# Two attention units from one 512-token load, all scores ahead of the first product with v, narrow idle matmuls first, and a last tile in three column pieces

## The chip, the cores and the metric

The kernel runs on one core of one Trainium2 chip. The metric is device time in microseconds (us); lower is better. Times are medians of several executions. Ratios are the mean time of one kernel's fast runs over that of the other's fast runs of the same rounds, so they are not quite the ratio of the medians quoted. A time is some 1.8 us longer than the span in the profile of the same run.

Words used below: TensorE (PE) does the matmuls and also loads their weights (PEld); VectorE is DVE, ScalarE is ACT, GpSimd is POOL. An *idle matmul* is one whose result nobody reads; it is there only to keep TensorE's clock up (run e8: with 25 of the 39 removed, the granted clock was at half from 12.4 to 19.2 us). *pv* is the product of the attention weights with v. *hps* is the hidden layer of the feed-forward part, *ops* its output layer.

## The reference, cut to what matters

```python
# attention inside chunks of 64 tokens, 8 heads of 64, then x @ w_in, a swish with a beta per column, @ w_out
scores = scale * np.matmul(q_c, k_c.transpose(0, 1, 2, 4, 3))
attn = np.exp(scores - max);  attn = attn / (sum + 1e-09)
x = np.matmul(attn, v_c)            # -> 4608 tokens x 512
h = x @ w_in                        # 512 -> 2048
g = h * (1.0 / (1.0 + np.exp(-beta * h)))
out = g @ w_out                     # 2048 -> 512
```

## The kernel before: the parts that matter

Tokens are handled in units of 256 (18 units) and blocks of two units (9 blocks). The order is written by hand. The beginning, with cuts:

```python
        # q, k of unit 0, heads 0-3: plain loads; heads 4-7: converting loads on the GpSimd queue
        for a, eng, dst in ((0, nc.sync, raw0), (1, nc.gpsimd, qk0[1])): ...   # runs of 512 B
        load_qk(1)                      # unit 1: two converting loads
        for i in range(4): load_v(i)
        ...                             # then w_in (8 loads), w_out, later units
        emit_idle(11, 512)              # 11 idle matmuls of 512 columns
        emit_T_half(0); emit_sc_half(0) # transpose on DVE, scores, exp
        emit_idle(3, 512)
        emit_T_half(1); emit_sc_half(1)
        ...
        emit_idle(13, 512)
        emit_T(1, ("qT", "kT")); emit_sc(1)
        emit_idle(4, 512)
        emit_pv(0); emit_norm(0, 0); emit_norm(0, 1)
        emit_idle(3, 512); emit_xt_pe(0, 0); emit_idle(3, 512); emit_xt_pe(0, 1); emit_idle(2, 512)
        emit_pv(1); emit_norm(1, 0); emit_norm(1, 1)
        a0, v0 = emit_m(0, 0, 0, 256, True)   # first hps group
```

In the middle, around units 4 and 5, `emit_T(5)` stands ahead of `emit_norm(4, ...)` on DVE, and `emit_sc(5)` ahead of `emit_t(1, 1, 0, 8)`. At the end the last 128 tokens are done in two halves of 256 columns, the second one evacuated by DVE and stored by ACT's queue.

The softmax here doesn't subtract the row's maximum and nothing guards it: scores larger than these inputs give would overflow.

## Time and profile before

| | before |
|---|---|
| median (lowest to highest of 5) | 291.94 us (291.58 to 292.25) |
| span in the profile | 290.0 us |
| TensorE busy | 283.1 us, 39 idle matmuls among it |
| first hps matmul | 16.03 us |
| first ops matmul | 31.11 us |

The first ops matmul is a good milestone: up to there every version here has done exactly the same useful work, so its start time tells what the head cost. The prediction below shows the busy rows, the stretches and the chain. The first row is the granted clock of TensorE in 40 slices of the span (9 is 90% or more); the others are the DMA queues with packets, megabytes and share of the 16 engines.

```profile
PEclk9999999999999999999999999999999999999999
...
q0 software_dynamic: 101216, 18.10, 84.2%
q1 hardware_dynamic: 40544, 18.24, 34.4%
q8 instruction: 21, 0.34, 0.5%
```

The clock is full in all slices. The third queue looks negligible and I passed over it: 21 packets, 0.34 MB, so 16 KB each. They are instructions.

### The profile page before, as it was taken

The page shows a single profiled execution, that of the slowest core. Times are in us where ns is not written, and L with a number is a line of the kernel's source. Part 1 is how long each engine was busy: PE and PEld are TensorE (multiplying, and loading weights), DVE is VectorE, ACT ScalarE, POOL GpSimd, SP SyncE. Part 2 cuts the span into 40 slices and gives each one's busy share as a digit, 9 for nine tenths or more (in the row PEclk, how much of TensorE's full clock was granted, in tenths as well). Part 3 has the DMA queues.
Part 4 walks back from the last instruction along what each step waited for, and adds up shares of the span by engine and source line. Part 5 has one row for each costly group of instructions (what it writes and reads, how often), then busy time and mean ns, then how long its engine had stood idle before and what let it go on. Part 6 is the DMA issues. An engine that isn't in the chain of part 4 may idle for free.

```text
span 290.0 us, 6476 instructions
## 1 busy us (share of the span) xinstructions
PE 283.1 (98%) x2695; PEld 135.5 (47%) x2695; DVE 139.8 (48%) x252; ACT 146.0 (50%) x224; POOL 97.5 (34%) x126
## 2 busy tenths in 40 slices
PE   7999999999999999999999999999999999999995
PEld 2464445545544444444444444444444444444444
DVE  3477444687366644534454444445453636433300
ACT  3277318783456645454545554455445544444411
POOL 8864569379152985070717070000000000000000
PEclk9999999999999999999999999999999999999999
DMA  9999999999969999999999999946346202100111
GB/s 143 170 196 205 177 176 212 211 161 158 133 98 135 200 168 144 168 151 156 135 123 171 118 158 113 198 65 92 91 107 78 75 36 72 38 36 36 38 72 72
DMA packets 141932, 36.86 MB, mean 127 GB/s; under 512 B 130000, under 2 KB 137424, under 8 KB 141904
## 3 DMA queue, kind: packets, MB, share of 16 engines
q0 software_dynamic: 101216, 18.10, 84.2%
q1 hardware_dynamic: 40544, 18.24, 34.4%
q8 instruction: 21, 0.34, 0.5%
q10 hardware_dynamic: 144, 0.13, 0.1%
q14 instruction: 7, 0.06, 0.1%
HBM read 36.71 MB, written 9.44 MB: 159 GB/s over the span
## 4 chain that ended last, share of the span: by engine, by line
PE 91%; DMA 2%; ACT 2%; DVE 2%; POOL 1%; issue 1%; DVEq 0%; ACTq 0%; POOLq 0%
PE hps L303 43%; PE ops L335 41%; DMA ku<-in_k_dram 2%; PE x L256 2%; PE sc L231 2%; PE sc L218 1%; PE ops L540 1%; ACT xt L288 1%; DVE x L271 1%; ACT sg L313 1%; PE warm L352 1%; POOL h L360 1%; PE xp L287 1%; DVE kT L154 0%; ACT osb L345 0%
## 5 line engine op out<-in xcount | busy, mean ns | idle before, releaser
L317 DVE SCALAR_TENSOR_TENSOR gt<-sg,hps 128x512 f16<-128x512 f32 (+1 forms) x152 | 99.2, 658 | 114.5 <-ACT sg L313 114.4
L313 ACT ACTIVATE sg<-hps,beta 128x512 f32<-128x512 f32 (+1 forms) x152 | 100.4, 665 | 74.7 <-PE hps L303 74.7
L303 PE MATMUL hps<-xt,win 128*128 128x512 f16 (+1 forms) x608 | 136.7, 368 | 0.4 <-ACT xt L288 0.2
L335 PE MATMUL ops<-wout,gt 128*128 128x512 f16 x560 | 131.1, 379 | 0.0
L303 PEld LDWEIGHTS <-win 128*128 128x128 f16 x608 | 57.6, 98 | 61.8 <-issue 0.9
L335 PEld LDWEIGHTS <-gt 128*128 128x128 f16 x560 | 53.8, 98 | 63.3
L345 ACT ACTIVATE osb<-ops 128x512 f32<-128x512 f32 x35 | 20.9, 598 | 44.4 <-PE ops L335 44.4
L110 POOL DMA_DIRECT2D vbig<-in_v_dram x40 | 34.2, 876 | 10.0 <-DMA wout<-in_moe_w_out_dram 4.3
L96 POOL DMA_DIRECT2D qu<-in_q_dram x22 | 18.7, 860 | 41.5 <-DMA qT<-qu 39.0
L271 DVE TENSOR_TENSOR x<-x,rd 128x512 f16<-128x512 f32 (+1 forms) x40 | 25.2, 637 | 1.4
L96 POOL DMA_DIRECT2D ku<-in_k_dram x22 | 18.8, 876 | 0.4 <-DMA ku<-in_k_dram 0.4
L240 ACT ACTIVATE et<-sc 128x1024 f16<-128x1024 f32 (+1 forms) x9 | 7.4, 834 | 10.2 <-PE sc L231 10.2
L352 PE MATMUL warm<-idle 128*128 128x512 f16 x39 | 11.2, 429 | 1.2 <-DVE braw L356 1.2
L267 DVE RECIPROCAL rd<-x 128x8 f32<-128x8 f32 x36 | 7.2, 200 | 8.8 <-PE x L256 8.8
L224 ACT ACTIVATE et<-sc 128x1024 f16<-128x1024 f32 x10 | 10.2, 1015 | 0.0
L256 PEld LDWEIGHTS <-et 64*64 64x64 f16 x576 | 6.1, 107 | 7.4 <-issue 3.8
L102 POOL DMA_DIRECT2D ku<-in_k_dram x10 | 7.7, 772 | 2.5 <-DMA win<-in_moe_w_in_dram 1.3
L102 POOL DMA_DIRECT2D qu<-in_q_dram x10 | 7.7, 781 | 2.4 <-DMA win<-in_moe_w_in_dram 1.4
L288 ACT COPY xt<-xp 128x512 f16<-128x512 f16 x12 | 6.7, 588 | 3.3 <-PE xp L287 3.3
L256 PE MATMUL x<-vbig,et 64*64 64x65 f16 x576 | 8.1, 195 | 0.0
L154 DVE STREAM_TRANSPOSE kT<-ku 128x512 f32<-128x512 f32 x7 | 5.0, 711 | 4.9 <-DMA ku<-in_k_dram 4.9
L553 DVE TENSOR_SCALAR osb<-ops 128x256 f32<-128x256 f32 x1 | 0.4, 424 | 12.5 <-PE ops L540 12.5
(34 smaller groups left out, 60.2 us busy)
## 6 DMA issues: line engine op xcount, KB each, us to landing
out_dram<-osb SPq DMA_DIRECT2D x35, 256.0 KB, 3.2
vbig<-in_v_dram POOLq DMA_DIRECT2D x32, 128.0 KB, 7.9
qu<-in_q_dram POOLq DMA_DIRECT2D x20, 128.0 KB, 6.6
ku<-in_k_dram POOLq DMA_DIRECT2D x20, 128.0 KB, 8.2
win<-in_moe_w_in_dram POOLq DMA_DIRECT2D x8, 256.0 KB, 9.2
wout<-in_moe_w_out_dram POOLq DMA_DIRECT2D x4, 512.0 KB, 12.2
qu<-in_q_dram POOLq DMA_DIRECT2D x4, 256.0 KB, 6.5
ku<-in_k_dram POOLq DMA_DIRECT2D x4, 256.0 KB, 7.3
```

Of the source, the lines that this page charges most:

```text
L96: nc.gpsimd.dma_start(out=tv[off:off + n, sp], in_=src[b, :, s:s + n, :].rearrange("h p d -> p h d"),)
L102: nc.gpsimd.dma_start(out=t[off // 2:(off + n) // 2], in_=src[b, :, s:s + n, :].rearrange("h (p r) d -> p h r d", r=2),)
L110: nc.gpsimd.dma_start(out=vbig[off:off + n, i, :, 0:D], in_=v[b, :, s:s + n, :].rearrange("h p d -> p h d"),)
L224: nc.scalar.activation(out=et, in_=sc, func=ACTF.Exp, scale=scale)
L256: nc.tensor.matmul(out=x[64 * c:64 * c + 64, r, g, 0:D + 1], lhsT=(et[64 * r:64 * r + 64, s, 4 * c + g, :] if u < XU else et[64 * r:64 * r ...
L271: nc.vector.tensor_tensor(out=o, in0=x[:, r, :, 0:D], in1=rd[:, r].to_broadcast(list(o.shape)), op=ALU.mult)
L303: nc.tensor.matmul(out=hps[:, 0:n], lhsT=w_in16[m // 2][:, kk, (m % 2) * 128:(m % 2) * 128 + 128], rhs=xr[:, c0 // CH:(c0 + n) // CH, 2 * ...
L313: nc.scalar.activation(out=sg[:, 0:n], in_=hps[:, 0:n], func=ACTF.Tanh, scale=beta2[:, m:m + 1])
L317: nc.vector.scalar_tensor_tensor(out=gt_t[j][:, m, c0:c0 + n], in0=sg[:, 0:n], scalar=1.0, in1=hps[:, 0:n], op0=ALU.add, op1=ALU.mult,)
L335: nc.tensor.matmul(out=ops, lhsT=gt_t[j][:, kk, t * 128:(t + 1) * 128], rhs=w_out16[kk // 4][:, kk % 4, :], start=(kk == 0), stop=(kk == K ...
L345: nc.scalar.activation(out=osb, in_=ops, func=ACTF.Copy, scale=0.5)
L352: nc.tensor.matmul(out=d[:, 0:w], lhsT=idle[:, 0:128], rhs=idle[:, 0:w])
```

## The change

The intent: fewer and longer runs in the first loads, so that everything behind them in the DMA queues comes earlier; fewer waits between the attention steps; a smaller last step. Cut to its core:

```diff
-    raw0 = [const.tile([128, HH, 2, D], FP32, ...)]          # unit 0 alone
+    raw0 = [const.tile([128, HH, 4, D], FP32, ...)]          # units 0 and 1, runs of 1 KB
...
-                nc.vector.tensor_copy(out=qk0[a][1], in_=raw0[1])
+                nc.scalar.copy(out=qk0[a][i], in_=raw0[i])    # both casts on ScalarE
...
-        load_qk(1)
...
-        emit_idle(11, 512)
+        emit_idle(78, 128)
         emit_T_half(0)
-        emit_sc_half(0)
-        emit_idle(3, 512)
+        emit_sc_half(0, 0); emit_ex_half(0, 0)
+        emit_idle(4, 512)
         emit_T_half(1)
-        emit_sc_half(1) ... emit_idle(13, 512) ... emit_sc(1) ... emit_idle(4, 512)
-        emit_pv(0) ... (idle matmuls 3, 3, 2 between the steps) ... emit_pv(1) ...
+        emit_sc_half(0, 1); emit_ex_half(0, 1)
+        emit_sc_half(1, 0); emit_sc_half(1, 1); emit_ex_half(1, 0, 2)
+        emit_pv(0, ("s", "p")); emit_norm(0, 0); emit_norm(0, 1)    # x halves in separate tiles
+        emit_pv(1, ("x", "p")); emit_norm(1, 1); emit_norm(1, 0)
+        emit_xt_pe(0, 0); emit_xt_pe(0, 1)
...
-        emit_T(5)
         emit_norm(4, 0); emit_norm(4, 1)
+        emit_T(5)
...
+        emit_t(1, 1, 0, 8)
         emit_sc(5)
-        emit_t(1, 1, 0, 8)
+        emit_t(1, 1, 8)
         emit_pv(5)
...
-        for hf in range(2):                                   # 256 + 256 columns
+        for c0, n in ((0, 256), (256, 128), (384, 128)):
```

## The prediction

> **What bounds the kernel now.** I read the page's busy table first, then the busy tenths, the chain of work that ended last, the timeline of the first 19 us, and last the chain around the few places where TensorE is not full.

> ```profile
> PE 283.1 (98%) x2695; PEld 135.5 (47%) x2695; DVE 139.8 (48%) x252; ACT 146.0 (50%) x224; POOL 97.5 (34%) x126
> ...
> PE   7999999999999999999999999999999999999995
> ```

> TensorE (PE) is busy 98% of the 290.0 us span, in every slice but the first and the last. So the change cannot pay in the middle unless it takes matmuls away, and it takes none of the useful ones. What is left is the head (until TensorE is full for good), the small gaps before 70 us, and the tail. The busy time hides that the head holds 39 idle matmuls, 11.2 us of work for nothing, which only keep the array awake. Cut into stretches:

> ```profile
> 0.00:19.00 19.00, 16.44 (x263) 8.18 (x264) 9.06 (x26) 7.65 (x14) 15.27 (x25) 1.00 1.47 167
> ...
> 43.00:52.00 9.00, 8.24 (x148) 4.82 (x147) 4.38 (x10) 6.85 (x14) 7.07 (x9) 1.00 1.84 209
> 52.00:62.00 10.00, 10.00 (x56) 5.34 (x55) 7.70 (x15) 7.71 (x14) 5.76 (x7) 1.00 1.85 190
> 62.00:70.00 8.00, 7.79 (x194) 4.18 (x193) 6.86 (x13) 4.71 (x9) 7.00 (x9) 1.00 2.11 145
> ```

> Columns: stretch, length, then busy us of PE, PEld, DVE, ACT, POOL. From 19.0 us on TensorE loses 0.76 us (43 to 52) and 0.21 us (62 to 70) before the tail, nothing else. The head is therefore worth most. Its chain:

> ```profile
> 2.89 0.85 POOL qu L102
> 3.74 6.45 DMA ku<-in_k_dram
> 10.21 0.72 DVE kT L154
> 10.98 0.71 PE sc L231 x64
> 11.69 0.97 PE warm L352 x4
> 12.66 0.28 PE x L256 x16
> ...
> 14.02 0.40 PE xp L287 x4
> 14.42 0.65 PE warm L352 x3
> 15.06 0.22 PE xp L287 x4
> 15.29 0.43 PE warm L352 x2
> ...
> 16.09 0.56 PE hps L303 x4
> ...
> 18.36 0.60 ACT xt L288
> ...
> 19.00 12.27 PE hps L303 x64
> ```

> The k load of unit 1 lands at 10.2 us and everything queues behind it; the first hidden-layer matmul (hps) comes at 16.0 and the unbroken stream at 19.0. Times of landing by tile say that two other things come just in time: the last of the four v loads lands at about 14.5, and the first w_in tile is issued at 8.8 and takes 7.2 us, so lands at 16.0, exactly when hps starts. The head is as much a DMA front as a chain of compute.

> [...] the first idle matmuls of 512 columns start 0.43 us apart until 4.65 us, later ones 0.22, and eight 128-column transposes at 75.54 take 0.45 us (56 ns each). [...] from its packet records, packets of 512 B on the plain load queue took 27 ns (about 600 a us over 16 engines); in the converting loads on the GpSimd queue one that writes 256 B took 41 ns (about 645 a us), one that writes 512 B (w_in) 60 ns (about 385 a us). Twice the bytes cost 1.5 to 1.7 times the time. [...] at 3.75 to 4.25 us plain packets fall away as those of the GpSimd queue come in.

> **The change part by part.**

> *Load.* q and k of units 0 and 1 were 1 MB in 512 B runs for unit 0 and 1 MB for unit 1, 4,096 packets. Now they are four loads with 1 KB runs of source, 2,048 packets. Before: 1,024 plain packets at 600 a us (1.7 us) and 3,072 converting ones at 645 a us (4.8 us), from 2.3 us to about 9.0, the last landing 10.2. After: 1,024 plain ones of 1 KB at an estimated 355 a us (45 ns each, as the 1 KB packets of the last output took) = 2.9 us, and 1,024 converting ones at 385 a us = 2.7 us; 5.6 us, so data end near 8.0 and the last k half lands near 9.0. **The DMA front moves up by about 1.1 us**, and v, w_in and all later loads, in the same queue, with it: last v near 13.4, w_in near 14.8.

> *Casts and transposes.* Both casts are now on ScalarE, 1,024 elements each: about 1.04 us, from 0.62 for 512 and the 1.02 against 0.60 of the exps. Four DVE transposes of 512 words at 0.71. Plain q lands near 4.2, plain k (now sharing engines with the GpSimd queue) near 6.5: cast to 7.6, transposed 8.3, first scores 8.4. 78 idle matmuls of 128 columns: 32 cold at 0.107 to 4.65 us, 46 at 0.056 = 2.6, ending 7.2, ahead of it. The second half: k lands 9.0, transposed 9.7.

> *Scores first.* Three score halves at 0.45 each: 9.75 to 11.1. Exp of half 1 to 10.9, of unit 1 11.1 to 12.1. pv(0) 11.1 to 11.6. Normalisation on DVE: 0.21 + 0.69 for the first half, then in two pieces 2 x (0.2 + 0.42) = 1.2: 11.4, 12.3, 13.5. pv(1) waits for exp (12.1) and for the last v (13.4), ends 13.6. The transposes of x stand behind it on TensorE, then two copies of 0.58 on ScalarE: hps starts at **about 15.1** instead of 16.0. The first w_in tile (14.8) would not allow much earlier. From there to the unbroken stream, 2.95 us before: three hps groups, two transposes, two copies behind each other on ScalarE; I get about 18.05. **Head: -0.95 us.** The 24 idle matmuls between took 0.22 each, but only 2.0 us of them stand in the chain, in places where it waited anyway for DVE and ScalarE.

> *Unit 4 and 5 order.* DVE normalises ahead of the transposes of unit 5 (2 x 0.6 us in the chain before the normalisation at 67.15). That removes the 0.21 us gap at 68.7; only 1.73 us of matmuls now cover the normalisation of unit 5 (1.8 us), giving 0.05 to 0.1 back. **-0.1 us.**

> *Tail.* 32 matmuls of 256 columns (3.51 us, 110 ns each) become 16 of 256 and 32 of 128 (56 ns): 1.76 + 1.79 = 3.55, **+0.04**. The last evacuation is half as wide: 0.42 to about 0.29 (slope from 0.69 at 512 and 0.42 at 256), **-0.13**; its store is 64 KB instead of 128 KB, 4 fewer packets an engine, **-0.1 to -0.2**. **Tail -0.25 us.**

> Sum: -0.95 - 0.1 - 0.25 = -1.3 us; 291.94 gives 290.6. I shade it to 290.5, because a front that moves more than I think is slightly likelier than one that moves less.

> **Rivals.** *The front does not move*: if plain and converting queues spoil each other, or landings are set by one late engine (v packets trickle to 14.5 us though most are through by 12.7), the last v and w_in land as before and hps starts at 16. For it: w_in lands in the same instant as hps starts. Against it: half the packets. Then 291.5 to 291.7. *The clock falls back*: from 11.6 to 15 us TensorE would have only pv(1) and a few transposes, where before idle matmuls filled the gaps. [...] *Compute bound head*: if v lands earlier than 12 us, pv(1), both transposes and copies move to DVE's pace and w_in sets the start: hps near 14.3, stream near 17.2, -2.1 in all: 289.8. *Loads become the bound later*: k of unit 2 lands 35.8, its transposes end 37.4, scores at 38.1: 0.7 us of slack. The front moves with TensorE, so I expect no wait.

> **Range and chances.** From 289.5 (compute-bound head and a good tail) to 291.6 (front unmoved). A 2% step would be 5.8 us; all that lies in head gaps and tail is less, as TensorE's useful work of about 272 us (283.1 - 11.2) stays. Faster by 2%: 0.01; within: 0.98; slower: 0.01.

> **What would show it.** Last half of k landing at 8.6 to 9.3 instead of 10.2; pv(1) held by v near 13.4; hps first at 14.8 to 15.4, unbroken from 17.7 to 18.4; the granted clock full from 4.65 us on; PE's gap at 62 to 70 gone; last evacuation 0.29 us. Wrong if hps starts before 14.3 or after 16, if hps matmuls of 256 columns take over 0.2 us each, or if TensorE gaps appear between 30 and 52 us beyond the 0.76 of before.

The forecast's sum: -0.95 - 0.1 - 0.25 = -1.3 us, so 290.6 from 291.94, shaded to 290.5. Idle matmuls of 128 columns at half clock start 0.107 us apart: a quarter of the 0.43 of 512 columns in the kernel before, and in the changed kernel, seen later, 0.107 us until 4.67 us and 0.056 after. In the quarters of a us from 3.50 to 4.25 us of the kernel before, 139, 60 and 9 plain packets start and 19, 80 and 113 of the GpSimd queue. That the idle matmuls keep the clock up is measured in e8.

## The result, and the profile after

The changed kernel takes 295.61 us (294.80 to 296.13, 5 runs) against 291.94 us: ratio 1.0123, 95% interval 1.0102 to 1.0144. That is slower, by 3.7 us, inside the 2% band, and outside the predicted range. The page of the changed kernel, its busy row, TensorE's tenths and the granted clock:

```profile
PE 281.8 (96%) x2754; PEld 139.8 (48%) x2754; DVE 140.5 (48%) x250; ACT 147.4 (50%) x225; POOL 95.6 (33%) x124
...
PE   8389999999999999999999899999999999999996
...
PEclk9959999999999999999999999999999999999999
```

TensorE has a hole in the second slice and a half clock in the third, neither of which was there before. The head from 11.6 us on in three stretches, first the kernel before, then the changed one (stretch, length, busy us of PE, PEld, DVE, ACT, POOL, then the granted clock, the DMA share and GB/s):

```profile
11.60:15.00 3.40, 3.28 (x60) 1.59 (x49) 1.83 (x6) 1.57 (x2) 2.17 (x4) 1.00 1.68 189
15.00:19.00 4.00, 3.86 (x63) 2.54 (x62) 2.83 (x9) 2.88 (x8) 2.62 (x5) 1.00 1.46 200
19.00:23.00 4.00, 4.00 (x27) 2.62 (x27) 2.58 (x6) 3.21 (x7) 2.07 (x4) 1.00 1.43 193
```

```profile
11.60:15.00 3.40, 0.08 (x9) 0.06 (x8) 0.00 (x0) 0.77 (x2) 1.48 (x3) 0.98 1.46 197
15.00:19.00 4.00, 2.80 (x63) 1.85 (x63) 3.54 (x12) 1.17 (x2) 2.62 (x4) 0.50 1.46 200
19.00:23.00 4.00, 3.76 (x26) 2.96 (x25) 1.12 (x4) 2.49 (x6) 1.79 (x4) 0.66 1.41 196
```

```profile
11.33 0.29 PE L262 MATMUL x<-vbig,et 64*64 64x65 f16 x13 [0.15 <-ACT et L204]
...
14.94 0.27 PE L262 MATMUL x<-vbig,et 64*64 64x65 f16 x3 [3.32 <-issue]
14.95 0.47 PE L262 MATMUL y<-vbig,et 64*64 64x65 f16 x16
```

The wait falls in the middle of sixteen alike matmuls that read the same v tile, and the profile names no releaser: "issue". The obvious suspect, a v load, had landed long before. The last two v loads of the changed kernel, from the view by tile:

```profile
L110 POOL DMA_DIRECT2D vbig<-in_v_dram x2: 923/928/933, 4.6 to 5.5; - x2
...
DMA to landing us min/median/max: 6.6/6.6/6.6
```

Issued at 4.6 and 5.5 us, landed at 11.2 and 12.1. So I counted TensorE's records: the matmul at 14.94 is preceded by exactly 449 of them, 447 matmuls and weight loads and two synchronising records at the start. And in the DMA packet records of the instruction queue the first 16 KB packet starts at 12.5 us, ends at 13.4, and TensorE goes on 1.5 us later.

The later parts behave as forecast in direction. The last evacuation, before and after, from the chain's end:

```profile
286.78 0.42 DVE osb L553
```

```profile
291.21 0.29 DVE osb L555
```

The time from the last matmul's start to the end of the span falls from 3.55 to 3.15 us.

**Theory A:** TensorE ran out of instructions. By this theory the instructions after the first 449 records come with the first 16 KB packet of the instruction queue (a *block* below), and this packet comes late, behind the data loads. That TensorE reads these packets is an inference: 21 of them serve a kernel (before) in which TensorE has 5,390 matmuls and weight loads, 257 a packet (an estimate, 5,390 / 21), while no other engine has more than 413 records there. 78 narrow idle matmuls with their weight loads are 156 instructions where 11 wide ones were 22. **Rival B:** a v load or another wait for data that the profile misnames. **Rival C:** the clock is the whole cause: the idle matmuls that kept it up between the steps are gone.

### The profile page after: what moved, and what is told of

The parts are those of the page before. It is cut to its first block, busy times and chain, and to the rows that moved or that the text cites. A ratio compares the mean times of both kernels' runs of the same rounds, so it can differ in the third digit from the quotient of the medians.

```text
span 294.1 us, 6595 instructions
## 1 busy us (share of the span) xinstructions
PE 281.8 (96%) x2754; PEld 139.8 (48%) x2754; DVE 140.5 (48%) x250; ACT 147.4 (50%) x225; POOL 95.6 (33%) x124
## 4 chain that ended last, share of the span: by engine, by line
PE 91%; ACT 2%; issue 2%; DVE 2%; DMA 2%; SPq 0%; DVEq 0%
PE hps L310 43%; PE ops L342 41%; PE x L262 2%; DMA raw<-in_k_dram 2%; PE sc L234 1%; PE sc L221 1%; PE ops L543 1%; ACT xt L295 1%; DVE t L175 1%; PE xp L294 1%; DVE x L278 1%; ACT osb L352 0%; ACT h L174 0%; ACT et L204 0%; PE sc L194 0%
## 5 line engine op out<-in xcount | busy, mean ns | idle before, releaser
L310 PEld LDWEIGHTS <-win 128*128 128x128 f16 x608 | 58.3, 99 | 64.2 <-issue 3.2
L352 ACT ACTIVATE osb<-ops 128x512 f32<-128x512 f32 x35 | 20.9, 598 | 42.2 <-PE ops L342 42.2
L96 POOL DMA_DIRECT2D qu<-in_q_dram x22 | 18.7, 862 | 45.2 <-DMA qT<-qu 35.2
L278 DVE TENSOR_TENSOR x<-x,rd 128x512 f16<-128x512 f32 x34 | 23.5, 691 | 1.3
L96 POOL DMA_DIRECT2D ku<-in_k_dram x22 | 18.8, 879 | 0.0
L276 DVE RECIPROCAL rd<-x 128x8 f32<-128x8 f32 x34 | 6.8, 201 | 15.4 <-PE x L262 15.4
L243 ACT ACTIVATE et<-sc 128x1024 f16<-128x1024 f32 (+1 forms) x8 | 6.4, 811 | 8.5 <-PE sc L234 8.5
L227 ACT ACTIVATE et<-sc 128x1024 f16<-128x1024 f32 x10 | 10.2, 1015 | 0.0
L359 PE MATMUL warm<-idle 128*128 128x128 f16 (+1 forms) x82 | 7.2, 264 | 1.2 <-DVE braw L363 1.2
L102 POOL DMA_DIRECT2D ku<-in_k_dram x9 | 6.8, 752 | 3.4 <-DMA win<-in_moe_w_in_dram 1.5
L102 POOL DMA_DIRECT2D qu<-in_q_dram x9 | 6.8, 761 | 2.5 <-DMA win<-in_moe_w_in_dram 1.3
L359 PEld LDWEIGHTS <-idle 128*128 128x128 f16 x82 | 6.3, 119 | 1.5 <-DVE braw L363 1.2
L555 DVE TENSOR_SCALAR osb<-ops 128x256 f32<-128x256 f32 (+1 forms) x2 | 0.7, 358 | 12.1 <-PE ops L543 12.1
## 6 DMA issues: line engine op xcount, KB each, us to landing
wout<-in_moe_w_out_dram POOLq DMA_DIRECT2D x4, 512.0 KB, 12.1
```

The lines of the kernel that those rows point to most:

```text
L96: nc.gpsimd.dma_start(out=tv[off:off + n, sp], in_=src[b, :, s:s + n, :].rearrange("h p d -> p h d"),)
L102: nc.gpsimd.dma_start(out=t[off // 2:(off + n) // 2], in_=src[b, :, s:s + n, :].rearrange("h (p r) d -> p h r d", r=2),)
L227: nc.scalar.activation(out=et, in_=sc, func=ACTF.Exp, scale=scale)
L278: nc.vector.tensor_tensor(out=o, in0=z[..., 0:D], in1=rd[:, r].to_broadcast(list(o.shape)), op=ALU.mult)
L310: nc.tensor.matmul(out=hps[:, 0:n], lhsT=w_in16[m // 2][:, kk, (m % 2) * 128:(m % 2) * 128 + 128], rhs=xr[:, c0 // CH:(c0 + n) // CH, 2 * ...
L352: nc.scalar.activation(out=osb, in_=ops, func=ACTF.Copy, scale=0.5)
```

## The experiments

Ten kernels; each was compared with the kernel before in its own rounds. "Stop after 449" gives the start of TensorE's 449th record, of any kind, and that of the next one, where a stop lies between. The last four columns come from one profiled execution of each kernel.

| run | edit | median us | ratio to before (95%) | instruction packet starts | stop after 449 | first hps | first ops |
|---|---|---|---|---|---|---|---|
| before | | 291.94 | | 12.2 | none | 16.03 | 31.11 |
| changed | | 295.61 | 1.0123 (1.0102-1.0144) | 12.5 | 11.4 to 14.94 | 18.40 | 34.68 |
| e1_wide20 | changed, 20 x 512 first | 293.59 | 1.0057 (1.0042-1.0072) | 14.2 | 13.7 to 16.65 | 17.69 | 33.61 |
| e4_mid41 | changed, 41 x 256 first | 294.96 | 1.0107 (1.0089-1.0125) | 14.3 | 13.0 to 16.64 | 18.78 | 34.74 |
| e2_before_88x64 | before, 88 x 64 first | 292.35 | 1.0013 (0.9995-1.0031) | 8.3 | none | 16.32 | 31.41 |
| e3_v_late | changed, v issued later | 295.74 | 1.0120 (1.0093-1.0147) | 9.2 | none | 19.74 | 36.47 |
| e5_early | changed, 90 x 64 and 5 x 512 first | 291.96 | 0.9998 (0.9977-1.0018) | 8.8 | none | 15.57 | 32.04 |
| e6_early_fill | e5 and 10 fill matmuls | 290.65 | 0.9954 (0.9941-0.9967) | 8.6 | 10.8 to 11.08 | 15.03 | 29.92 |
| e7_before_mid_tail | before, reorder and tail alone | 291.31 | 0.9988 (0.9964-1.0012) | 12.0 | none | 18.32 | 33.40 |
| e8_before_nofill | before without 25 idle matmuls | 292.50 | 1.0024 (1.0008-1.0041) | 14.7 | under 0.1, if any | 15.22 | 31.62 |
| e9_narrow_fill | changed and 10 fill matmuls | 295.29 | 1.0128 (1.0101-1.0154) | 12.8 | 11.5 to 15.20 | 20.22 | 35.11 |
| e10_sc_early | e6, scores of unit 1 earlier | 290.46 | 0.9962 (0.9940-0.9984) | 9.0 | 10.7 to 11.33 | 15.03 | 29.92 |

### e1_wide20 and e4_mid41: the same idle time in fewer instructions

```diff
-        emit_idle(78, 128)
+        emit_idle(20, 512)        # e1;  e4: emit_idle(41, 256)
```

> The changed kernel with 20 idle matmuls of 512 columns first in place of 78 of 128: the same 6.1 us of idle work, 116 fewer TensorE instructions. Theory A (instruction supply: TensorE stops after 449 of its instructions because the next 16 KB block of instructions waits behind the data loads): the stop moves 116 instructions later in the program, to the first hidden-layer matmul, and the 3.3 us gap at 11.6 us goes or shrinks below 0.7; hidden layer starts near 15.1, time 290.5 to 291.5. Rival B (TensorE waits for a v load): v loads are untouched, gap stays, 295 to 296. Rival C (the clock alone falls back because the idle matmuls between the steps are gone): no gap changes; the half-rate stretch of 6.8 us stays, 295 or so.

> The changed kernel with 41 idle matmuls of 256 columns first (same 6.1 us, 74 fewer instructions than with 78). Theory A: TensorE again stops after its 449th instruction, which is now inside the second half of pv of unit 1 (near 12.4 us); pv of unit 0 and its normalisation are through by then, so about 1 us less is lost up to the stop; it ends near 14.9 as before; hidden layer near 16.2, time between the two others, about 292 to 293.5. Rivals B and C: as the changed kernel, 295 to 296.

TensorE's waits in the head, e1 and then e4 (engine, line, releaser, total us, times, longest):

```profile
PE xp L294 <- issue: 3.1, 1, 3.1
```

```profile
PE y L262 <- issue: 3.4, 1, 3.4
```

The stop is again a wait for nothing that the profile shows, and in both it stands before the 450th record: at another instruction of the program (an x transpose in e1, pv of unit 1 in e4), but at the same count. (The count holds when waits for semaphores are counted too: 445 matmuls and weight loads and 4 other records in e1, 446 and 3 in e4, 447 and 2 in the changed kernel.) That is what theory A said and what rival B cannot say, since three different places of the program, one of which reads no v, stop at one number. The size I expected was wrong, though: the stop hardly shrank (2.9 and 3.7 us from record to record, against 3.5), and e4's time (294.96) lies beside the 295 of rivals B and C. It is the place of the stop that decides here, not the time. The packet, too, came later, at 14.2 and 14.3 us, instead of staying at 12.5. Why was not shown; the guess is that with fewer idle instructions ahead TensorE is behind in its stream, and the packet with it. (No record shows what sets the packet off: in e7 it started when only 175 of TensorE's records had begun, in the changed kernel when all 449 had.) e1 is 2 us faster than the changed kernel all the same. 1.07 us of this stand at the first ops matmul, where more work is through before the stop; e1's trace also lacks a later wait of 1.2 us (see "Later loads" below). e4 gains nothing in the head (34.74 against 34.68).

### e2_before_88x64: many narrow matmuls in the kernel before

```diff
-        emit_idle(11, 512)
+        emit_idle(88, 64)
```

> The kernel before with one edit: its first 11 idle matmuls of 512 columns become 88 of 64 (same time, 154 more TensorE instructions). Theory A: the 449th instruction is now near the end of the scores of unit 1 (11.6 us); if the block of instructions comes no earlier than in the changed kernel, TensorE stops there until about 14.5: 2 to 3 us slower, 294 to 295. If the earlier request is served earlier, less. Rivals B and C: nothing else is changed and the gaps are still filled, so 291.9 as before.

The stop that the first part of the expectation feared did not come, and this taught most: 154 more instructions, and no stop. The packet starts at 8.3 us, has landed when the 449th instruction is through at 11.7, and the time is the same within the interval. The number of instructions alone is not the cause. What counted here is whether the packet had landed when the 449th record was through, and with many instructions *early* the packet started early, at 8.3 us against 12.2 in the kernel before. (The "request" is what sets the packet off; the traces show only its start.) (Rivals B and C forecast this time too; e2 alone does not decide between them and A.)

### e3_v_late: the DMA engines emptied first

```diff
-        for i in range(4): load_v(i)
         make_identity(nc, ident)
+        nc.gpsimd.tensor_copy(out=gate, in_=qk0[1][1][:, 0, 0, 0:1])   # waits for the last k half
+        for i in range(4): load_v(i)
```

> The changed kernel with 78 narrow matmuls, but the four v loads are issued only once the last k half has landed (near 8.7 us)[...]. Theory A with queueing: the block's packet starts near 9.6 instead of 12.5 us and the gap after the 449th instruction goes or becomes one of v (pv waits for v, 12 to 13 us); the v loads and w_in then land 1 to 2 us later, hidden layer near 16 to 17, time 292.5 to 294.5. [...] Rival B: later v makes it worse, over 296.

The stream up to there is the changed kernel's, instruction for instruction on TensorE; only the v packets are out of the way. The packet starts at 9.2 instead of 12.5 us and the stop is gone. TensorE now waits for v, and says so:

```profile
12.30 0.32 PE L262 MATMUL x<-vbig,et 64*64 64x65 f16 x16 [1.15 <-DMA vbig<-in_v_dram]
...
17.61 0.43 PE L262 MATMUL y<-vbig,et 64*64 64x65 f16 x16 [2.02 <-DMA vbig<-in_v_dram]
```

So the loads queued then (the edit holds back v and, behind it, w_in) had made the block 3.3 us late, and these real waits for v are named by the profile, unlike the stop. The time, 295.74, is above the 292.5 to 294.5 I expected: v came later than I had thought, and the clock was at half here too.

### e5_early and e6_early_fill: the packet early; then also the clock kept

```diff
-        emit_idle(78, 128)
+        emit_idle(90, 64)
+        emit_idle(5, 512)
# e6 in addition: emit_idle takes an existing tile, and
-        emit_idle(4, 512)
+        fill = emit_idle(6, 512)
...
         emit_norm(0, 1)
+        emit_idle(2, 512, fill)
         emit_pv(1, ("x", "p"))
...
         emit_xt_pe(0, 0)
+        fill = emit_idle(2, 512)
         emit_xt_pe(0, 1)
+        emit_idle(4, 512, fill)
```

> The changed kernel whose first idle work is 90 matmuls of 64 columns and then 5 of 512 (190 instructions in about 6 us instead of 156)[...]. Theory A (the stop is a late block of instructions[...]): the block's packet starts by 9 us as in the run before with 88 narrow ones (8.3), lands by 11.3, and the 3 us stop after instruction 449 is gone although there are more instructions than in the changed kernel; hidden layer starts near 15 if the clock holds. A plain count of instructions (more is worse) says a stop as long or longer and 295 or more. Clock (theory C) may still fall to half in one or two windows, so 291 to 293.

> e5 with 10 more idle matmuls of 512 columns put where TensorE waits (2 ahead of the second score half, 2 after pv of unit 0, 2 and 4 around the second x transpose). If the half clock is caused by too little wide work in a window, it stays full here and hidden-layer matmuls of 256 columns take 0.11 us apiece: stream near 17.9 instead of 19.0, and with the reorder (-0.38) and the tail (-0.3) 290.0 to 290.6, faster than both kernels. If the clock falls all the same, as e5.

Both did as expected, e6's time lying 0.05 us above its range. With 34 more instructions than the changed kernel, e5 has no stop, and gains back 3.65 us (2.64 at the first ops matmul; its trace, too, lacks the later wait of 1.2 us). Its clock is still at half for 6.8 us, and its hidden-layer matmuls show it; e6, with ten idle matmuls more, runs them at full speed. e6 has a small stop again, of 0.26 us ahead of its 450th record. First e5, then e6, the first two hidden-layer groups (eight matmuls of 256 columns):

```profile
15.57 1.87 PE L310 MATMUL hps<-xt,win 128*128 128x256 f16 x8 [0.67 <-ACT xt L295]
```

```profile
15.03 1.04 PE L310 MATMUL hps<-xt,win 128*128 128x256 f16 x8
```

e6 beats both kernels, by 1.3 us the one before. Its head chain is now what the prediction had described for the changed kernel: the last v load sets the pace, the hidden layer starts at 15.0, the unbroken stream at 17.8.

```profile
5.46 7.52 DMA vbig<-in_v_dram
...
15.20 0.87 PE hps L310 x8
...
17.82 1.25 PE hps L310 x10
```

(e6's profile holds no clock records, so its clock is read off the matmuls here; its page and its other runs give 0.999 to 1.0.)

### e9_narrow_fill: the fourth corner

```diff
 # e6 with the changed kernel's first idle matmuls
-        emit_idle(90, 64)
-        emit_idle(5, 512)
+        emit_idle(78, 128)
```

> The changed kernel with its 78 narrow first matmuls and with the ten fill matmuls of the run that beat both kernels: the fourth corner of stop x clock. If stop and clock are separate causes, the stop after instruction 449 stays (the block's packet near 12.5 us, the gap to 14.9) and only part of the clock loss goes, since the stop itself leaves a window of 3.4 us nearly without work: 293 to 295.5, first output matmul at 33 to 34.7 us where the changed kernel has 34.7 and the run with early request and fill 29.9. If the clock was the cause of all, 290.7.

The stop stays where it was, with all fill in place, and the time with it. The clock falls inside the stop (half from 13.0 to 19.9 us by its clock records):

```profile
15.20 0.27 PE L262 MATMUL x<-vbig,et 64*64 64x65 f16 x5 [3.51 <-issue]
```

So the fill alone saves nothing: the stop comes first and takes the clock with it. With e5 and e6 this closes the square: 295.6 (stop, no fill), 295.3 (stop, fill), 292.0 (no stop, no fill), 290.65 us (fill, and of the stop 0.26 us left).

### e8_before_nofill: the clock by itself

```diff
-        emit_idle(13, 512)
-        emit_idle(4, 512)         # ahead of pv(0)
-        emit_idle(3, 512)  (twice)
-        emit_idle(2, 512)
```

> The kernel before without the 25 idle matmuls between its attention steps (13, 4, 3, 3, 2), the first 11 and the 3 kept. Theory C measured by itself: the clock drops to half for one or two windows of 3.4 us between 8 and 19 us; matmuls of 256 columns in the head take 0.21 us; 1 to 2.5 us slower, 293 to 294.5, with no stop without a reason in the trace. If the clock holds without the idle work, 291.8 or a little less, and the changed kernel's half clock comes from its stop alone.

In the kernel before, without a stop, the clock falls to half from 12.4 to 19.2 us when the idle matmuls are taken away. The net loss was smaller than expected, 0.55 us in the median: without idle matmuls in the way the hidden layer starts 0.8 us earlier (15.22 against 16.03), and still the first ops matmul is 0.5 us later. From hps to ops it takes 16.40 us instead of 15.08, so the half clock costs about 1.3 us there (an estimate from these four times).

### e7_before_mid_tail: the later parts alone

```diff
# kernel before, with the reorder of units 4 and 5 and the three column pieces of the changed kernel
```

> The kernel before with the reorder of units 4 and 5 and the three-piece tail alone. By the two traces: the reorder gives -0.38 us, the tail -0.29: 291.1 to 291.4 where before is 291.8 to 291.9. If those gains belong to the late start of the changed kernel (loads better ahead of TensorE), only the tail's 0.3 remains.

By the time it is unclear: the interval includes 1. The profiled run, the slowest of six at 293.35, had its first loads late and one window at half clock in the head. From scores to scores the trace tells more. From the scores of unit 2 to those of unit 8 it takes 61.47 us, and 61.84 to 61.86 in the three traces with the old order (before, e2, e8); the traces of the changed kernel and of the runs built on it give 61.46 to 61.47 (e9 alone 61.70). The reorder gives 0.38 us in all but one of them. The tail's step from last matmul to end is 3.15 against 3.55, less 0.04 for the matmuls.

### e10_sc_early: one step more

```diff
         emit_ex_half(0, 0)
+        emit_sc_half(1, 0)
-        fill = emit_idle(6, 512)
+        fill = emit_idle(5, 512)
...
-        emit_sc_half(1, 0)
         emit_sc_half(1, 1)
```

> The run with early request and fill (290.65), with the first score half of unit 1 moved ahead of the second half load's scores, in place of one idle matmul: the exp of unit 1 can start 0.4 us earlier. If pv of unit 1 waits for the exp, 0.1 to 0.3 us faster (290.4); if it waits for the last v load (0.27 us in that trace) or the normalisation on DVE sets the start of the hidden layer, the same, 290.6.

No gain in the head: the first hps and ops matmuls start at the same hundredth. The earlier use of instructions made e6's small stop longer, 0.68 us from record to record, again ahead of the 450th:

```profile
11.33 0.23 PE L194 MATMUL sc<-t,t 32*64 32x64 f16 x5 [0.49 <-issue]
```

It was hidden there by other waits.

Over all twelve traces: in the six with a stop (changed, e1, e4, e6, e9, e10; 0.3 to 3.7 us long, with the packet's start between 8.6 and 14.3 us) TensorE goes on 1.4 to 1.6 us after the block's packet has ended, whether it ended at 9.5 or at 15.3 us. In five of the other six the packet had ended at least 1.9 us before the 450th record; in e8 it ended 1.4 us before, on the edge.

## Why the prediction was wrong, point by point

**The step that failed** is the sentence "hps starts at **about 15.1** instead of 16.0", and the sum built on it, "Head: -0.95 us". The chain behind it was right as a chain of data: e6 starts hps at 15.03. It lacked one supply, TensorE's own instructions. In the changed kernel hps started at 18.40: TensorE stood still for 3.3 us before it, and the clock was at half after that. Two of the prediction's own signs of being wrong came true, hps after 16 us and hps matmuls of 256 columns at 0.21 us each.

**The sum with its true terms**, at the first ops matmul, where all have done the same useful work. Instruction stop: changed less e5, 34.68 - 32.04 = +2.64 us. Half clock: e5 less e6, 32.04 - 29.92 = +2.12. What the loads and the new order give when neither is in the way: e6 less before, 29.92 - 31.11 = -1.19. Together +3.57, which is 34.68 - 31.11. The first two are taken in this order; as e9 shows, the stop by itself also brings the clock down, so in the changed kernel they are not independent.

**The clock rival** was in the prediction and was set aside there. It came true, in the changed kernel (half from 14.87 us) and without a stop in e5, which fell to half after a window (9.82 to 13.24 us) with 1.76 us of matmul work in it, and stayed there for two windows, 6.8 us; that cost 2.12 us at the first ops matmul (e5 less e6). (The prediction's reading that the clock of the kernel before rose at 4.65 us is off: its clock records say 4.41.)

**The load front** moved as said, and further. Last v at 12.1 us (13.4 predicted, about 14.5 before), first w_in issued at 6.92 and landed 7.6 us later at 14.5 (14.8 predicted). Expected "pv(1) held by v" shows in e6, at 12.98, not in the changed kernel, where the stop outlasted v.

**Casts and transposes.** The casts took 1.05 us as estimated. The DVE transposes were mis-sized: taken as 0.71 us for 512 words, measured at 1.08 with four tokens to a partition instead of two (that this is the cause was not tested). The kernel before, then the changed one (count, busy us, mean ns):

```profile
L154 DVE STREAM_TRANSPOSE qT<-qu 128x512 f32<-128x512 f32 x1 | 0.7, 715 | 0.7 <-DMA qu<-in_q_dram 0.7
```

```profile
L175 DVE STREAM_TRANSPOSE t<-h 128x512 f32<-128x512 f32 x4 | 4.1, 1084 | 3.7 <-ACT h L174 3.7
```

The first scores still came at 8.32 (8.4 predicted) because two errors cancelled: k landed earlier, at 6.1 instead of 6.5. The second half had no such luck: its scores came at 10.17, 9.75 predicted.

**The reorder** was right in direction, too small in size: -0.1 predicted, -0.38 measured. **The tail** as well: -0.25 predicted; 0.40 less 0.04 is -0.36. One reason given for it was wrong: the last store has 128 packets as before, not fewer; each is half as long and took 26 ns instead of 45.

**Later loads**: k of unit 2 made no wait, as said. But in the profiled run of the changed kernel one hidden-layer group at 162.50 us waited for its input, which comes by a DMA transpose: issued at 156.3, it took 6.1 us to land, against at most 4.0 in the same stage before. It cost 1.2 us (scores to scores, 60.30 against 59.11), so 1.2 of the 4.1 us that this run lost arise outside the head. The profile calls this wait "issue" too. e6's trace has such a wait of 0.9 us, the other traces have none; which executions have it stays open. With it the spans add up: 3.57 - 0.38 + 1.2 - 0.36 = 4.0, against 294.05 - 289.96 = 4.1.

**Open**: what sets an instruction packet off, and why it started 3.3 us later with the v loads queued (12.5 us in the changed kernel, 9.2 in e3). What separates windows that lose the clock from those that keep it also stays open: by the clock records, windows with 1.94 us of TensorE time (e8) and 2.26 (e10) kept it, windows with 0.96 (e8), 1.76 (e5), 2.11 (e4) and 2.32 (e1) lost it, so busy time alone does not decide. Once at half, the clock stayed there for one window (3.4 us, e7), two (6.8 us: changed, e5, e8, e9) or three (10.2 us: e3, e4).

## What to carry to other kernels

Instructions can be an input too. Here TensorE stopped after 449 records in six of twelve traces, for 0.3 to 3.7 us, while loads filled the DMA queues; where a kernel loads as heavily at its start, count TensorE's records up to a wait without a reason, and look when the packets of the instruction queue start. A wait that the profile calls "issue", in the middle of alike instructions (3.3 us in the changed kernel), was the sign here (the word "issue" alone is not: the wait at 162 us has it and was one for data). Narrow idle work *first* brought the block in time here (e2, e5: packet at 8.3 and 8.8 us) or nearly (e6: 8.6); wide idle work alone moved the stop and did not remove it (e1, e4: still 2.9 and 3.7 us). Look at the granted clock before idle work is taken out of the gaps between small matmuls: in e8 it fell to half for 6.8 us.
